# Sliding-window attention on 64-wide TensorE tiles instead of block-diagonal 128-wide operands

## Chip, cores and metric

One core of one Trainium2 chip. The metric is the device time of one execution in microseconds (us); with one core there is no slowest core to choose. Times are medians with the lowest and highest run. The *span* is the profiled part of an execution, some 2 us shorter than its time. Engines: PE is TensorE's matmuls, PEld its weight loads, DVE is VectorE, ACT ScalarE, POOL GpSimd, SP SyncE; L209 is line 209 of a kernel.

## The reference, cut to what matters

```python
# attention: 8 batches, 8 heads, 576 tokens, head size 64, window 64
scores = (q @ k^T) / sqrt(64)
mask = (rel >= 0) & (rel < 64)                   # rel = query position - key position
attn = softmax(where(mask, scores, -1e9))
x = (attn @ v).transpose(0, 2, 1, 3).reshape(4608, 512)
# feed-forward
g = x @ w_gate                                   # 512 -> 1536
out = (silu(g) * (x @ w_val)) @ w_out            # 1536 -> 512
```

A query sees at most 64 keys, so a block of 64 keys matters only to two blocks of 64 queries: its own and the next. The kernel takes the 4608 tokens in nine tiles of 512 (eight key blocks), and two heads at a time (four *pairs* per tile).

## The kernel before

Two heads share the 128 partitions. To keep them apart the keys lie block-diagonally (kbd), and so do the values (vbd): half of each 128x128 operand is zeros, written once by memsets. One matmul then gives the scores of one key block for both heads, with head on the partitions.

```python
def transposes(t, u):
    tp = ps_a.tile([P, 2, 512], BF16, name="tp", tag="a")
    # ... eight 128x128 transposes of the cast queries and keys into tp
    nc.scalar.copy(queries[t][:, u, :], tp[:, 0, :])                 # qT, ACT
    kt = tp[:, 1, :].rearrange("r (j e x) -> r j e x", j=8, e=2)
    for a in range(2):                                               # kbd, DVE, twice
        r = slice(64 * a, 64 * a + 64)
        kb = kbd[t % 2][r, u, :, r].rearrange("r j (x e) -> r j e x", e=2)
        nc.vector.tensor_copy(kb, kt[r])

def masks(t, u, eng=nc.gpsimd):
    # ... two multiplications of E by the mask, on eng
    if t < 8:
        nc.gpsimd.memset(E[:, t, 0, :], 0.0)                         # batch boundary
    F = epool.tile([P, 8, 64], BF16, name="F", tag="F")
    nc.gpsimd.tensor_add(F[:], E[:, :, 0, :], E[:, :, 1, :])         # for the denominators

def attention(t, after):            # tiles 0 and 1 only
    casts(t)
    for u in range(4):
        for g in range(2):
            cast_unit(nc.gpsimd, t, 0, g, u=u)       # q_b on POOL
            cast_unit(nc.vector, t, 1, g, u=u)       # k_b on DVE
        transposes(t, u)
        cast_v(t, u)
        if u == 3:
            after()                                  # POOL issues weight transfers
        if u:
            scores(t, u - 1)
            masks(t, u - 1, nc.vector)
        if u > 1:
            products(t, u - 2)
    # ... scores and masks of pair 3, products of pairs 2 and 3

attention(0, lambda: weights_gv(0, 384))
nc.vector.memset(kbd[1][:], 0.0)
nc.vector.memset(vbd[1][:], 0.0)
nc.vector.memset(vbd[2][:], 0.0)
for m in range(3):
    gate_value(0, m)
# ... attention(1), gate work of both tiles, then
for u in range(4):
    transposes(2, u)
    if u == 0:
        project(0, 0)
    scores(2, u); cast_v(2, u); masks(2, u, nc.vector)
    if u:
        project(0, u)
cast_qk(3)                                           # eight casts on POOL
for u in range(4):
    transposes(3, u); products(2, u); project(1, u); scores(3, u)
# ... and the steady part, t = 3 to 8:
for u in range(4):
    products(t, u)
    if u % 2 == 0:
        project(t - 1, u // 2)
for u in range(4):
    scores(t + 1, u)
    if u % 2 == 1:
        project(t - 1, 2 + u // 2)
```

tp, s_ps (scores), ad_ps (denominators) and ao_ps (products) share four PSUM banks, the pool ps_a.

The softmax here doesn't subtract the row's maximum and nothing guards it: scores larger than these inputs give would overflow.

## Time and profile before

| | before |
|---|---|
| time | 415.82 us (415.72 to 418.97, 3 runs) |
| span | 413.7 us |
| PE / DVE / ACT / POOL busy | 359.3 / 200.5 / 187.5 / 190.3 us |

The prediction shows five stretches of the table of windows, the steady tile and the chain. Two more readings are needed below. First the stretches again, cut this time at instructions that both kernels have (the gate run that waits for the last xT, the first key cast of tile 1, the first transposes after the gate work). Columns: window and length, then busy us and instruction count of PE, PEld, DVE, ACT, POOL, then granted clock (the share of TensorE's full speed that was granted), DMA share, GB/s.

```profile
0.00:36.58 36.58, 14.89 (x107) 10.04 (x108) 18.29 (x33) 12.95 (x22) 18.17 (x39) 1.00 0.77 159
36.58:46.11 9.53, 6.29 (x25) 2.49 (x24) 7.04 (x7) 3.57 (x5) 3.13 (x6) 0.83 0.36 94
46.11:73.82 27.71, 14.22 (x112) 10.41 (x112) 14.14 (x29) 11.89 (x21) 17.89 (x30) 0.50 0.96 174
...
109.43:153.54 44.11, 35.78 (x282) 20.32 (x281) 23.85 (x37) 17.73 (x32) 16.94 (x29) 0.92 0.30 90
153.54:214.14 60.60, 59.89 (x386) 31.05 (x383) 31.97 (x47) 31.95 (x52) 42.76 (x58) 1.00 0.57 127
214.14:252.39 38.25, 37.55 (x260) 19.92 (x257) 19.65 (x29) 20.89 (x34) 23.43 (x32) 1.00 0.47 111
```

They are attention of tile 0, the early gate work, attention of tile 1, then (after a PE-full stretch of 35.61 us, left out) attention of tiles 2 and 3 between projections, and two stretches where PE is full. Only the first four stretches are not bound by PE.

Second, the timelines of PE and POOL of the kernel before where tile 3 begins (start, busy us, instruction, and in brackets the idle time before it and what ended it):

```profile
128.57 4.28 PE L268 MATMUL o_ps<-wo,hT 128*128 128x512 bf16 x12
...
137.18 3.40 PE L268 MATMUL o_ps<-wo,hT 128*128 128x512 bf16 x12
```

```profile
129.66 0.15 POOL L211 MEMSET E<- 128x64 bf16 x1 [2.95 <-DVE E L209]
130.14 1.14 POOL L213 TENSOR_TENSOR F<-E 128x512 bf16<-128x512 bf16 x1 [0.34 <-DVE E L209]
131.23 0.61 POOL L118 CAST q_b<-q_f 128x512 bf16<-128x512 f32 x1
```

The projection o_ps takes 2.75 us elsewhere in this kernel; these two run partly at a halved clock (granted clock 0.50 from 128.26 to 131.67 and from 135.09 to 138.50 us). POOL waits 2.95 us for masked weights E, does a memset and F, and only then the casts on which tile 3's transposes wait.

### The profile page before, as it was taken

How to read it: one execution, taken by the hardware profiler on the slowest of the kernel's cores; microseconds unless marked ns; L12 is line 12 of the kernel's file. 1: busy time of each engine (PE TensorE's matmuls, PEld its weight loads, DVE VectorE, ACT ScalarE, POOL GpSimd, SP SyncE). 2: the span in 40 equal slices, each digit the busy share in tenths (PEclk: the TensorE clock that was granted, in tenths of full speed). 3: DMA queues.
4: the chain of work that ended last, by engine and by line, in shares of the span. 5: the costliest groups of instructions: out<-in, count | busy, mean ns of one | idle time of the engine just before them, and what ended most of it. 6: DMA issues, size and time to landing. Idle time of an engine off the chain costs nothing.

```text
span 413.7 us, 6332 instructions
## 1 busy us (share of the span) xinstructions
PE 359.3 (87%) x2296; PEld 189.2 (46%) x2296; DVE 200.5 (48%) x300; ACT 187.5 (45%) x306; POOL 190.3 (46%) x281
## 2 busy tenths in 40 slices
PE   2177445999957999999999999999999999999996
PEld 0153234444533565455455455544555554454442
DVE  4466654433453465662654456346526543343332
ACT  0355325433431465475456546644754565353320
POOL 6163269400046159769626945691599029400000
PEclk9999555999998899999999999999999999999999
DMA  8648499997010919313921671193123011002002
GB/s 213 146 93 150 109 224 158 207 225 143 16 52 26 253 67 232 87 53 106 198 53 52 174 154 50 58 251 81 36 84 86 0 52 51 2 26 78 0 2 101
DMA packets 88415, 42.89 MB, mean 104 GB/s; under 512 B 41280, under 2 KB 83776, under 8 KB 88384
## 3 DMA queue, kind: packets, MB, share of 16 engines
q1 hardware_dynamic: 78304, 36.19, 36.0%
q0 software_dynamic: 5792, 4.72, 7.4%
q10 hardware_dynamic: 4288, 1.57, 1.8%
q8 instruction: 18, 0.29, 0.3%
q14 instruction: 13, 0.11, 0.1%
HBM read 37.75 MB, written 9.44 MB: 114 GB/s over the span
## 4 chain that ended last, share of the span: by engine, by line
PE 77%; SPq 7%; DMA 7%; ACT 2%; POOL 2%; DVE 2%; issue 2%; ACTq 0%; POOLq 0%
PE g_ps L257 22%; PE v_ps L257 22%; PE o_ps L268 21%; DMA k_f<-in_k_dram 4%; PE ao_ps L233 4%; SPq L91 4%; PE tp L158 3%; PE s_ps L191 3%; SPq L101 2%; PE ad_ps L224 2%; DVE kbd L170 2%; DMA q_f<-in_q_dram 2%; ACT E L196 1%; DMA v_f<-in_v_dram 1%; SPq L86 1%
## 5 line engine op out<-in xcount | busy, mean ns | idle before, releaser
L263 DVE TENSOR_TENSOR hT<-sg,v_ps 128x512 bf16<-128x512 f32 x108 | 74.1, 687 | 92.3 <-PE v_ps L257 87.8
L257 PE MATMUL v_ps<-xT,wv 128*128 128x512 bf16 x432 | 111.7, 381 | 2.9 <-DVE hT L263 2.9
L257 PE MATMUL g_ps<-xT,wg 128*128 128x512 bf16 x432 | 112.3, 382 | 0.2 <-DVE xT L242 0.2
L262 ACT ACTIVATE sg<-g_ps 128x512 f32<-128x512 f32 x108 | 64.4, 597 | 105.3 <-PE g_ps L257 105.2
L268 PE MATMUL o_ps<-wo,hT 128*128 128x512 bf16 x432 | 100.7, 385 | 0.0
L209 POOL TENSOR_TENSOR E<-E,mask 128x512 bf16<-128x512 bf16 x48 | 54.3, 1152 | 35.0 <-ACT E L196 33.4
L170 DVE COPY kbd<-tp 64x512 bf16<-64x512 bf16 x72 | 52.2, 725 | 35.6 <-ACT qT L165 35.1
L257 PEld LDWEIGHTS <-wv 128*128 128x128 bf16 x432 | 42.3, 98 | 55.4 <-issue 4.2
L257 PEld LDWEIGHTS <-wg 128*128 128x128 bf16 x432 | 41.8, 99 | 47.4 <-issue 1.1
L268 PEld LDWEIGHTS <-hT 128*128 128x128 bf16 x432 | 40.8, 99 | 45.3 <-issue 2.8
L213 POOL TENSOR_TENSOR F<-E 128x512 bf16<-128x512 bf16 x36 | 41.6, 1156 | 16.6 <-DVE E L209 14.5
L196 ACT ACTIVATE E<-s_ps 128x512 bf16<-128x512 f32 (+1 forms) x72 | 37.7, 594 | 25.0 <-PE s_ps L191 24.9
L165 ACT COPY qT<-tp 128x512 bf16<-128x512 bf16 x36 | 21.1, 587 | 49.6 <-PE tp L158 49.6
L242 DVE TENSOR_TENSOR xT<-ao_ps,r 128x512 bf16<-128x512 f32 x36 | 26.3, 731 | 25.3 <-ACT r L241 19.6
L118 POOL CAST q_b<-q_f 128x512 bf16<-128x512 f32 x28 | 17.2, 613 | 46.1 <-PE tp L158 46.1
L158 PE MATMUL tp<-identb,q_b 128*128 128x128 bf16 x144 | 17.2, 238 | 21.1 <-POOL q_b L120 19.2
L211 POOL MEMSET E<- 128x64 bf16 x32 | 4.8, 150 | 56.5 <-DVE E L209 55.3
L233 PEld LDWEIGHTS <-vbd 128*128 128x128 bf16 x320 | 23.3, 108 | 14.6 <-issue 9.2
L239 ACT ACTIVATE ld<-ad_ps 128x512 f32<-128x512 f32 x36 | 21.6, 599 | 18.5 <-PE ad_ps L224 18.3
L191 PE MATMUL s_ps<-qT,kbd 128*128 128x128 bf16 (+1 forms) x288 | 23.9, 232 | 4.2 <-DVE kbd L170 4.1
L233 PE MATMUL ao_ps<-E,vbd 128*128 128x128 bf16 x320 | 25.6, 234 | 0.0
L191 PEld LDWEIGHTS <-kbd 128*128 128x128 bf16 x288 | 19.5, 108 | 13.1 <-DVE kbd L170 8.0
(72 smaller groups left out, 251.7 us busy)
## 6 DMA issues: line engine op xcount, KB each, us to landing
q_f<-in_q_dram SPq DMA_DIRECT2D x9, 512.0 KB, 5.0
k_f<-in_k_dram SPq DMA_DIRECT2D x9, 512.0 KB, 7.4
v_f<-in_v_dram SPq DMA_DIRECT2D x16, 112.0 KB, 2.8
v_f<-in_v_dram SPq DMA_DIRECT2D x12, 128.0 KB, 3.3
wg<-in_moe_w_gate_dram POOLq DMA_DIRECT2D x4, 384.0 KB, 8.1
wv<-in_moe_w_val_dram POOLq DMA_DIRECT2D x4, 384.0 KB, 10.2
v_f<-in_v_dram SPq DMA_DIRECT2D x16, 96.0 KB, 3.9
wo<-in_moe_w_out_dram POOLq DMA_DIRECT2D x2, 768.0 KB, 23.8
```

Source lines behind the costliest of these rows:

```text
L158: nc.tensor.transpose(tv[:, i, g, e], x[:, g, e, 2 * u:2 * u + 2, :].rearrange("r h d -> r (h d)"), identb[:],)
L170: nc.vector.tensor_copy(kb, kt[r])
L191: nc.tensor.matmul(s_ps[:, 64 + P * i:64 + P * i + n], kbd[t % 2][:, u, j, :], qT[:, 64 * j:64 * j + n],)
L196: nc.scalar.activation(Ef[:, 512 * h + lo:512 * h + 512], s_ps[:, lo:512], AF.Exp, scale=0.125)
L209: eng.tensor_mul(part, part, mf[:, lo:512])
L213: nc.gpsimd.tensor_add(F[:], E[:, :, 0, :], E[:, :, 1, :])
L233: nc.tensor.matmul(o_ps[:, lo:hi], vb, Ef[:, e0:e0 + hi - lo], start=first, stop=(j == 7), skip_group_check=True,)
L242: nc.vector.tensor_mul(xT[t][:, u, :].rearrange("r (j x e) -> r j e x", j=8, e=2), o_ps[:].rearrange("r (j e x) -> r j e x", j=8, e=2), r[ ...
L257: nc.tensor.matmul(ps[:], w[:, c, P * m:P * m + P], xT[t][:, c, :], start=(c == 0), stop=(c == 3),)
L262: nc.scalar.activation(sg[:], g_ps[:], AF.Silu)
L263: nc.vector.tensor_mul(hT[t][:, m, :], sg[:], v_ps[:])
L268: nc.tensor.matmul(o_ps[:], hT[t][:, c, P * s:P * s + P], wo[:, c, :], start=(c == 0), stop=(c == 11),)
```

## The change

The intent: use TensorE's quadrants, so that nothing is stored block-diagonally. Keys stay dense (kT, one copy); each score matmul uses 64 rows (one head) and 64 columns of TensorE (a *TensorE tile*, printed as 64*64 in the traces below; tiles that have all rows and half of the columns, printed as 128*64, are *column tiles*), and the parity of the key block decides which half of the partitions it writes. Each head then has its own PSUM bank and its keys on the partitions, two neighbouring key blocks one above the other. The products contract over all 128 partitions for a 64-query block, so the denominator is a matmul with ones, and F goes. The zero halves and their memsets go.

```diff
-    kbd = [... [P, 4, 8, P] ...]      # 2
-    vbd = [... [P, 4, 8, P] ...]      # 3
+    kT = [... [P, 4, 512] ...]        # 2
+    vp = [... [P, 9, H, D] ...]       # 2; POOL writes each value block to two slots
@@ transposes
-        nc.scalar.copy(queries[t][:, u, :], tp[:, 0, :])
-        for a in range(2): ... nc.vector.tensor_copy(kb, kt[r])
+        nc.scalar.copy(outs[0], parts[0])            # now reorders on write
+        nc.vector.tensor_copy(outs[1], parts[1])
@@ scores
-        per half: 1 + 4 matmuls with kbd[:, u, j, :], N = 64 or 128
+        for j in range(-1 if t else 0, 8):
+            c = j % 2
+            for h in range(2):
+                r = slice(64 * h, 64 * h + 64)
+                nc.tensor.matmul(s_ps[h][64 * c:64 * c + 64, lo:hi],
+                                 src[r, u, 64 * (j % 8):64 * (j % 8) + 64], qT[r, lo:hi])
+        tile 0 only: a memset and a small exponential per head for the first block
@@ masks
-        two multiplications of 512 columns
-        if t < 8: nc.gpsimd.memset(E[:, t, 0, :], 0.0)
-        nc.gpsimd.tensor_add(F[:], E[:, :, 0, :], E[:, :, 1, :])
+        one multiplication of 1024 columns
+        if 0 < t < 8:
+            a = 64 * (1 - t % 2)
+            nc.gpsimd.memset(E[a:a + 64, :, 64 * t:64 * t + 64], 0.0)
@@ products
-        nc.tensor.matmul(d_ps[:], bones[:], F)
-        9 matmuls with vbd, accumulating
+        for h in range(2):
+            nc.tensor.matmul(d_ps[64 * h:64 * h + 64, :], ones[:], E[:, h, :])
+        for m in range(8):
+            for h in range(2):
+                nc.tensor.matmul(o_ps[64 * h:64 * h + 64, 64 * m:64 * m + 64],
+                                 vp[t % 2][:, m, 2 * u + h, :], E[:, h, 64 * m:64 * m + 64])
@@ between attention of tile 0 and its gate work
-    nc.vector.memset(kbd[1][:], 0.0); nc.vector.memset(vbd[1][:], 0.0); nc.vector.memset(vbd[2][:], 0.0)
```

Value transfers change shape too, and those of tiles 0 and 1 are issued with the first pair.

More of the change, by code (lines that the diff above doesn't have):

```diff
@@ L47 @@
     wo = cst.tile([P, 12, DM], BF16, name="wo")
-    kbd = [cst.tile([P, 4, 8, P], BF16, name=f"kbd{i}") for i in range(2)]
-    vbd = [cst.tile([P, 4, 8, P], BF16, name=f"vbd{i}") for i in range(3)]
+    kT = [cst.tile([P, 4, 512], BF16, name=f"kT{i}") for i in range(2)]
+    vp = [cst.tile([P, 9, H, D], BF16, name=f"vp{i}") for i in range(2)]
     identb = cst.tile([P, P], BF16, name="identb")
-    bones = cst.tile([P, P], BF16, name="bones")
-    mask = cst.tile([P, 4, 2, 64], BF16, name="mask")
+    ones = cst.tile([P, D], BF16, name="ones")
+    mask = cst.tile([P, 2, 4, 2, 64], BF16, name="mask")
     def segments(t):
@@ L95, in load_qk, with load_v @@
                 o, s, left = o + m, s + m, left - m
-    def load_v(engs, t, p):
-        v_f = stage.tile([P, 8, D], FP32, name="v_f", tag="v_f", bufs=8)
-        for off, b, s0, n in segments(t):
-            for a in range(2):
-                engs[a].dma_start(
-                    v_f[64 * a:64 * a + 64, off // 64:(off + n) // 64],
-                    v[b, 2 * p + a, s0:s0 + n].rearrange("(j r) d -> r j d", r=64),
-                )
-        staged[t, p] = v_f
+    def load_v(engs, t, by_head=False):
+        v_f = stage.tile([P, 4, H, D], FP32, name="v_f", tag="v_f")
+        staged[t, "v"] = v_f
+        n = 0
+        for off, b, s0, left in segments(t):
+            o, s = off, s0
+            while left:
+                m = min(left, P - o % P)
+                if by_head and m == P:
+                    m = left // P * P
+                    for h in range(H):
+                        engs[h % 2].dma_start(
+                            v_f[:, o // P:(o + m) // P, h, :],
+                            v[b, h, s:s + m].rearrange("(i r) d -> r i d", r=P),
+                        )
+                else:
+                    engs[n % 2].dma_start(
+                        v_f[o % P:o % P + m, o // P],
+                        v[b, :, s:s + m].rearrange("h r d -> r h d"),
+                    )
+                n += 1
+                o, s, left = o + m, s + m, left - m
     ready = {}
@@ L130, in cast_qk, with cast_v @@
                     cast_unit(nc.gpsimd, t, i, g, e=e)
-    def cast_v(t, p):
-        v_f = staged.pop((t, p))
-        vb = vbd[t % 3]
-        nc.gpsimd.tensor_copy(vb[0:64, p, :, 0:64], v_f[0:64])
-        nc.gpsimd.tensor_copy(vb[64:128, p, :, 64:128], v_f[64:128])
+    def cast_v(t, u):
+        v_f = staged[t, "v"]
+        hs = slice(2 * u, 2 * u + 2)
+        if u == 0 and t:
+            nc.gpsimd.tensor_copy(vp[t % 2][64:128, 0], vp[(t - 1) % 2][64:128, 8])
+        for a in range(2):
+            r = slice(64 * a, 64 * a + 64)
+            dst = vp[t % 2][r, a:a + 8, hs, :].rearrange("r (i c) h d -> r i c (h d)", c=2)
+            src = v_f[r, :, hs, :].rearrange("r i h d -> r i (h d)")
+            nc.gpsimd.tensor_copy(
+                dst, src.rearrange("r i (c x) -> r i c x", c=1).broadcast_to([64, 4, 2, P])
+            )
     def weights_gv(f0, f1):
@@ L164, in transposes @@
             queries[t] = att.tile([P, 4, 512], BF16, name="qT", tag="qT")
-        nc.scalar.copy(queries[t][:, u, :], tp[:, 0, :])
-        kt = tp[:, 1, :].rearrange("r (j e x) -> r j e x", j=8, e=2)
-        for a in range(2):
-            r = slice(64 * a, 64 * a + 64)
-            kb = kbd[t % 2][r, u, :, r].rearrange("r j (x e) -> r j e x", e=2)
-            nc.vector.tensor_copy(kb, kt[r])
+        parts = [tp[:, i, :].rearrange("r (j e x) -> r j e x", j=8, e=2) for i in range(2)]
+        outs = [
+            x[:, u, :].rearrange("r (j x e) -> r j e x", j=8, e=2)
+            for x in (queries[t], kT[t % 2])
+        ]
+        nc.scalar.copy(outs[0], parts[0])
+        nc.vector.tensor_copy(outs[1], parts[1])
     weights = {}
@@ L176, in scores @@
         qT = queries[t][:, u, :]
-        E = epool.tile([P, 8, 2, 64], BF16, name="E", tag="E")
-        Ef = E[:].rearrange("r m c x -> r (m c x)")
-        for h in range(2):
-            s_ps = ps_a.tile([P, 512], FP32, name="s_ps", tag="a")
-            lo = 0
-            if t == 0 and h == 0:
-                lo = 64
-            else:
-                j = 4 * h - 1
-                kb = kbd[t % 2][:, u, j, :] if j > 0 else kbd[(t - 1) % 2][:, u, 7, :]
-                nc.tensor.matmul(s_ps[:, 0:64], kb, qT[:, 256 * h:256 * h + 64])
-            for i in range(4):
-                n = P if i < 3 else 64
-                j = 4 * h + i
-                nc.tensor.matmul(
-                    s_ps[:, 64 + P * i:64 + P * i + n],
-                    kbd[t % 2][:, u, j, :],
-                    qT[:, 64 * j:64 * j + n],
-                )
-            nc.scalar.activation(
-                Ef[:, 512 * h + lo:512 * h + 512], s_ps[:, lo:512], AF.Exp, scale=0.125
-            )
+        E = epool.tile([P, 2, 512], BF16, name="E", tag="E")
+        s_ps = [ps_a.tile([P, 512], FP32, name="s_ps", tag="a") for _ in range(2)]
+        for j in range(-1 if t else 0, 8):
+            c = j % 2
+            lo, hi = max(0, 64 * j), min(512, 64 * j + P)
+            src = kT[t % 2] if j >= 0 else kT[(t - 1) % 2]
+            for h in range(2):
+                r = slice(64 * h, 64 * h + 64)
+                nc.tensor.matmul(
+                    s_ps[h][64 * c:64 * c + 64, lo:hi],
+                    src[r, u, 64 * (j % 8):64 * (j % 8) + 64],
+                    qT[r, lo:hi],
+                )
+        for h in range(2):
+            if t == 0:
+                nc.vector.memset(E[64:128, h, 0:64], 0.0)
+                nc.scalar.activation(E[0:64, h, 0:64], s_ps[h][0:64, 0:64], AF.Exp, scale=0.125)
+            lo = 0 if t else 64
+            nc.scalar.activation(E[:, h, lo:512], s_ps[h][:, lo:512], AF.Exp, scale=0.125)
         weights[t, u] = E
@@ L203, in masks @@
         E = weights[t, u]
-        Ef = E[:].rearrange("r m c x -> r (m c x)")
-        mf = mask[:].rearrange("r m c x -> r (m c x)")
-        for h in range(2):
-            lo = 64 if t == 0 and h == 0 else 0
-            part = Ef[:, 512 * h + lo:512 * h + 512]
-            eng.tensor_mul(part, part, mf[:, lo:512])
-        if t < 8:
-            nc.gpsimd.memset(E[:, t, 0, :], 0.0)
-        F = epool.tile([P, 8, 64], BF16, name="F", tag="F")
-        nc.gpsimd.tensor_add(F[:], E[:, :, 0, :], E[:, :, 1, :])
-        weights[t, u] = (E, F)
+        eng.tensor_mul(
+            E[:].rearrange("r h x -> r (h x)"),
+            E[:].rearrange("r h x -> r (h x)"),
+            mask[:].rearrange("r h i c x -> r (h i c x)"),
+        )
+        if 0 < t < 8:
+            a = 64 * (1 - t % 2)
+            nc.gpsimd.memset(E[a:a + 64, :, 64 * t:64 * t + 64], 0.0)
     xT = {}
     def products(t, u):
-        E, F = weights.pop((t, u))
-        Ef = E[:].rearrange("r m c x -> r (m c x)")
+        E = weights.pop((t, u))
         if u == 0:
@@ L223, in products @@
         d_ps = ps_a.tile([P, 512], FP32, name="ad_ps", tag="a")
-        nc.tensor.matmul(d_ps[:], bones[:], F[:].rearrange("r m x -> r (m x)"))
+        for h in range(2):
+            nc.tensor.matmul(d_ps[64 * h:64 * h + 64, :], ones[:], E[:, h, :])
         o_ps = ps_a.tile([P, 512], FP32, name="ao_ps", tag="a")
-        first = True
-        for j in range(-1, 8):
-            if j < 0 and t == 0:
-                continue
-            vb = vbd[t % 3][:, u, j, :] if j >= 0 else vbd[(t - 1) % 3][:, u, 7, :]
-            lo, hi = max(0, 64 * j), min(512, 64 * j + P)
-            e0 = 64 * (2 * j + 1) if j >= 0 else 0
-            nc.tensor.matmul(
-                o_ps[:, lo:hi], vb, Ef[:, e0:e0 + hi - lo],
-                start=first, stop=(j == 7), skip_group_check=True,
-            )
-            first = False
+        for m in range(8):
+            for h in range(2):
+                nc.tensor.matmul(
+                    o_ps[64 * h:64 * h + 64, 64 * m:64 * m + 64],
+                    vp[t % 2][:, m, 2 * u + h, :],
+                    E[:, h, 64 * m:64 * m + 64],
+                )
         ld = fsb.tile([P, 512], FP32, name="ld", tag="ld", bufs=2)
@@ L241, in products @@
         nc.scalar.activation(r[:], ld[:], AF.Exp, scale=-1.0)
-        nc.vector.tensor_mul(
-            xT[t][:, u, :].rearrange("r (j x e) -> r j e x", j=8, e=2),
-            o_ps[:].rearrange("r (j e x) -> r j e x", j=8, e=2),
-            r[:].rearrange("r (j e x) -> r j e x", j=8, e=2),
-        )
+        nc.vector.tensor_mul(xT[t][:, u, :], o_ps[:], r[:])
     hT = {}
@@ L290, in loads_v @@
     def loads_v(t):
-        for p in range(4):
-            load_v((nc.sync, nc.sync), t, p)
+        load_v((nc.sync, nc.sync), t)
     def loads_by_head(t, e0, e1):
@@ L299, in loads_by_head @@
                 load_qk(e1, t, 1, 2 * u + a)
-            load_v((e0, e1), t, u)
+            if u == 0:
+                load_v((e0, e1), t, by_head=True)
     loads_by_head(0, nc.sync, nc.scalar)
@@ L307 @@
     make_identity(nc, identb[:])
-    nc.vector.memset(kbd[0][:], 0.0)
+    nc.vector.memset(ones[:], 1.0)
+    nc.vector.memset(vp[0][64:128, 0], 0.0)
     nc.gpsimd.memset(mask[:], 1.0)
-    nc.vector.memset(vbd[0][:], 0.0)
-    nc.vector.memset(bones[:], 0.0)
-    nc.vector.memset(bones[0:64, 0:64], 1.0)
-    nc.vector.memset(bones[64:128, 64:128], 1.0)
     for a in range(2):
-        half = mask[64 * a:64 * a + 64].rearrange("r m c (e x) -> r m c e x", e=2)
-        nc.gpsimd.affine_select(
-            out=half[:, :, 0], in_=half[:, :, 0], compare_op=ALU.is_ge, fill=0.0,
-            base=-1, pattern=[[0, 4], [-1, 2], [-2, 32]], channel_multiplier=1,
-        )
-        nc.gpsimd.affine_select(
-            out=half[:, :, 1], in_=half[:, :, 1], compare_op=ALU.is_ge, fill=0.0,
-            base=0, pattern=[[0, 4], [1, 2], [2, 32]], channel_multiplier=-1,
-        )
+        for h in range(2):
+            half = mask[64 * a:64 * a + 64, h]
+            nc.gpsimd.affine_select(
+                out=half[:, :, 1 - a], in_=half[:, :, 1 - a], compare_op=ALU.is_ge, fill=0.0,
+                base=-1, pattern=[[0, 4], [-1, 64]], channel_multiplier=1,
+            )
+            nc.gpsimd.affine_select(
+                out=half[:, :, a], in_=half[:, :, a], compare_op=ALU.is_ge, fill=0.0,
+                base=0, pattern=[[0, 4], [1, 64]], channel_multiplier=-1,
+            )
     def attention(t, after):
@@ L346 @@
     set_silu()
-    nc.vector.memset(kbd[1][:], 0.0)
-    nc.vector.memset(vbd[1][:], 0.0)
-    nc.vector.memset(vbd[2][:], 0.0)
     for m in range(3):
```

## The prediction

> **What bounds the kernel now.** I read the table of stretches first: each engine's busy time in windows, cut where the chain of waits changes character. Columns: window and length, busy us and instruction count of PE, PEld, DVE, ACT, POOL, granted clock, DMA share, GB/s.
>
> ```profile
> 0.00:35.00 35.00, 13.50 (x103) 9.52 (x104) 17.57 (x32) 11.42 (x20) 18.17 (x39) 1.00 0.75 155
> ...
> 44.00:72.56 28.56, 14.80 (x117) 10.84 (x116) 14.09 (x29) 10.65 (x20) 16.80 (x28) 0.50 0.90 168
> 72.56:109.38 36.82, 36.81 (x168) 16.42 (x167) 14.49 (x21) 14.28 (x23) 4.13 (x8) 0.99 0.90 165
> 109.38:153.00 43.62, 35.30 (x273) 19.84 (x272) 23.36 (x36) 17.66 (x31) 16.40 (x28) 0.92 0.31 91
> ...
> 253.22:291.47 38.25, 37.54 (x257) 19.90 (x256) 19.65 (x29) 20.89 (x35) 23.41 (x33) 1.00 0.43 111
> ```
>
> So there are two kernels in one. In the two stretches before 72.6 us no engine is over 60% busy: attention of tiles 0 and 1 is a chain of short steps from engine to engine. From 72.6 to 109.4, and from about 137 to the end, PE is full (37.54 of 38.25 us in a tile), and only PE work counts. Between 109.4 and about 137 PE is held up again. Second view, the timeline of PE in a steady tile:
>
> ```profile
> 217.39 0.38 PE L224 MATMUL ad_ps<-F,bones 128*128 128x512 bf16 x1
> 217.61 0.61 PE L233 MATMUL ao_ps<-E,vbd 128*128 128x64 bf16 x9
> ...
> 222.03 0.19 PE L187 MATMUL s_ps<-qT,kbd 128*128 128x64 bf16 x1
> 222.06 0.36 PE L191 MATMUL s_ps<-qT,kbd 128*128 128x128 bf16 x4
> 222.25 0.19 PE L187 MATMUL s_ps<-qT,kbd 128*128 128x64 bf16 x1
> ...
> 223.58 0.19 PE L187 MATMUL s_ps<-qT,kbd 128*128 128x64 bf16 x1 [0.70 <-ACT E L196]
> ```
>
> By start times, a head pair's denominator takes 0.22, its products 0.45, its scores 2 x 0.22 = 0.45 us; one wait of 0.70 us per tile comes in the scores. So attention's products and scores cost 4 x (0.67 + 0.45) = 4.5 of 38.25 us; the rest is FFN and transposes. Third, the chain of waits (start, us, piece) around 126 us, and the timeline of the start:
>
> ```profile
> 125.86 0.59 ACT qT L165
> 126.48 0.71 DVE kbd L170
> 127.20 0.74 DVE kbd L170
> ...
> 128.45 1.09 ACT E L196 x2
> ...
> 130.17 0.13 POOL F L213
> ...
> 131.23 0.61 POOL q_b L118
> ```
>
> ```profile
> 43.53 1.86 PE L257 MATMUL v_ps<-xT,wv 128*128 128x512 bf16 x4 [2.92 <-DVE hT L263]
> ...
> 59.08 1.15 POOL L213 TENSOR_TENSOR F<-E 128x512 bf16<-128x512 bf16 x1 [0.21 <-DVE E L209]
> ...
> 60.17 0.86 POOL L120 CAST q_b<-q_f 128x256 bf16<-128x256 f32 x2
> ```
>
> Two key copies of 0.73 us, one after the other, lie on the path of every head pair in the short-step stretches; the F add on POOL (1.15 us) stands in front of the query casts for the next pair or tile; and PE waits 2.92 us for an hT multiply that stands behind three DVE memsets of 1.76 us.
>
> [...] No tiled matmul is in this trace.[...] 0.03 us from a 64-column matmul to the next.[...]
>
> **The change, part by part.** I follow the instruction order of both kernels per engine.
>
> *Start, to 72.6 us.* ACT does its first copy at 13.05 us, after issuing its loads and a table load; unchanged. In tile 0 I redid the trace's chain with the new lengths: one key copy of 0.73 for two; no F before the next query cast; but two extra small exponentials per pair on ACT (two heads' first 64 rows; my estimate from 597 against 548 ns for 512 and 448 columns: about 0.25 each), and both heads' scores are interleaved, so the first exponential waits for both. The gain of 1.3 to 1.9 us per pair is mostly given back to ACT: I get about 1.4 us. Then three DVE memsets (3 x 1.76, with pauses to 6.4 us) vanish between tile 0's attention and its first hT: worth the 2.92 us wait and a bit, 3.3. In attention of tile 1 the loop of 5.8 us per pair (query cast at 54.41, again at 60.17) loses F and half of the key copy but keeps a POOL memset: about 1 us in each of two loops, and 0.3 in the first. At the end POOL issues the remaining weight transfers (62.20 to 68.35) before the last masks' follow-up: one F of 1.15 goes, while the value casts before it double (64x512 at 0.61 each, 2 per pair, become 64x1024, estimate 1.2 each: +1.2). Together 1.4 + 3.3 + 2.3 + about 1 = 8 us. SP issues 58 instead of 64 transfers for tile 1 (about 0.47 us each), so loads don't hold it back much, though the last keys land near when they are wanted.
>
> *Stretch 109 to 137.* Four pairs each lose 0.73 of the key copy: 2.9. The last one loses F before the eight casts for tile 3: 1.15. Back come perhaps 0.2 for the interleaved scores: about 4 us saved.
>
> *PE-bound remainder.* Scores become 18 matmuls per pair (64 rows, 64 columns of weights, N = 128 or 64) for 10; products 16 (N = 64) for 9; denominators 2 for 1: PE goes from 2296 to 2872 matmuls. The work in columns is 2 x 1024 for scores on four tiles: a perfect overlap gives 0.21 us for 0.45. Products: 1024 columns on two column tiles: 0.21 for 0.45. Denominators 2 x 512 on two: 0.22 as before. Best case 0.47 us per pair less, 1.9 per tile. If instead each load-and-matmul pair takes 27 ns whatever the tile, scores are 0.49 and products 0.43, nothing gained.[...] I choose about 20 to 24 ns: -0.6 per tile.[...] The wait at the second score pair remains, and more matmuls now stand behind it (18 instead of 5): +0.25. So +0.25 per tile, times 6 tiles of such work, +1.5 us[...].
>
> *Beside other work, no time:* the key copies from 72 to 36 (26 us of DVE), F (41.6 us of POOL) against longer value casts (+43 us), masks merged into half as many instructions of twice the length, fewer value transfers, and everything in the steady tile that isn't PE: DVE, ACT and POOL are 50 to 60% busy there.
>
> Sum: -8 - 4 + 2.5 = -9.5 us on a span of 413.7; the measured time is 2.1 us above the span: 415.8 - 9.5 = about 406.
>
> **Rivals.** (a) Tiles overlap ideally: PE saves up to 1.9 - 0.9 = 1 us per tile, 6 us more: about 398.[...] Against:[...] here each matmul has its own weight load. (b) Weight loads or a lack of overlap bind:[...] (c) The start is held by transfers (DMA share 0.75 and 0.90) and weights come too late when the start gets shorter: the 8 us shrink to 3 or 4, giving about 410. Against: in 44 to 72 the chain is engine steps, and PE waits for weights only 0.9 us in all. (d) The POOL value casts become the bound: 4 x 2.4 + 0.6 + casts 4.5 + masks 9.1 + memsets 0.6 = 24.4 us of POOL per tile, against 23.4 before in 38.25: no.
>
> **Range and chances.** The early gain is fairly sure (12, give or take 3)[...]. So 395 to 419 at 8 in 10. Faster by over 2% (below 407.5) needs a PE term below about +4: 0.57. Slower by over 2% needs rival (b) nearly in full: 0.07. The rest, 0.36.
>
> **What would show it.** In the changed profile: first gate matmul run of tile 1 (72.56 before) at about 64.5; the stretch from the end of the early gate work to the PE-full part shorter by 4 us; a tile period near 38.5 for 38.25; scores of a pair 0.3 to 0.5 us and products 0.3 to 0.45 by start times; POOL about as busy as before, DVE about 26 us less. A tile period over 40 means that loads or mode changes cost far more than I took; under 37.5 that tiles overlap nearly fully. A start that is no shorter means that the loads or ACT set it.

The sum came to -9.5 us: -8 at the start, -4 in the stretch of tiles 2 and 3, +2.5 for the rest. What a change of mode (full array to TensorE tiles or back) was taken to cost had no measurement behind it; it was part of the +0.25 per tile, of the 0.9 in rival (a) and of the +2.5, so what is printed of these does not add up. The 0.21 us of perfect overlap and the 27 ns are estimates from the trace of before: four gate matmuls of 512 columns are followed by the next group after 0.86 us, so 0.215 us each, and 27 ns for 64 columns. The 20 to 24 ns are between these 27 ns and the 12 to 13 ns that 0.21 us for 18 or 16 matmuls comes to.

## The result

| | before | after |
|---|---|---|
| time | 416.34 us (415.72 to 418.97, 4 runs) | 403.09 us (402.35 to 403.85, 4 runs) |
| span | 413.7 us | 400.5 us |
| mean granted clock | 0.955 | 0.964 |
| DVE busy | 200.5 us | 165.9 us |

The ratio is 0.967 (95% interval 0.9623 to 0.9717): faster by 3.3%. All ratios here are the mean time of one kernel's fast runs over that of the other's fast runs of the same rounds, so not quite the ratio of the quoted medians. The engine line of the page of after, and its clock by slices in tenths (40 slices of 10 us):

```profile
PE 352.9 (88%) x2872; PEld 173.4 (43%) x2872; DVE 165.9 (41%) x254; ACT 193.1 (48%) x314; POOL 186.0 (46%) x229
...
PEclk9999559999997999999999999999999999999999
```

PE runs 576 matmuls more and is busy 6.4 us less. The two slices at 5 are attention of tile 1, where PE is busy half of the time (11.84 of 23.56 us), and the 7 is the beginning of tile 3 (granted clock 0.50 from 119.27 to 126.10 us). The table of stretches of after, cut at the same instructions as that of before:

```profile
0.00:31.90 31.90, 13.40 (x171) 7.43 (x172) 13.65 (x30) 13.73 (x30) 21.49 (x38) 1.00 0.81 184
31.90:38.30 6.40, 5.91 (x25) 2.49 (x24) 1.98 (x4) 3.24 (x5) 2.82 (x4) 1.00 0.33 91
38.30:61.86 23.56, 11.84 (x175) 7.01 (x176) 11.03 (x21) 12.43 (x22) 16.24 (x27) 0.57 0.87 180
...
97.63:140.03 42.40, 34.99 (x378) 18.00 (x375) 17.13 (x25) 18.46 (x31) 15.33 (x25) 0.92 0.29 94
140.03:200.90 60.87, 59.78 (x449) 29.62 (x448) 26.96 (x40) 33.23 (x52) 41.56 (x45) 1.00 0.51 126
200.90:239.24 38.34, 37.24 (x322) 18.54 (x320) 16.65 (x25) 21.60 (x34) 22.63 (x26) 1.00 0.43 111
```

Length against length: 36.58 to 31.90 (-4.7), 9.53 to 6.40 (-3.1), 27.71 to 23.56 (-4.2), the PE-full stretch 35.61 to 35.77 (+0.2), 44.11 to 42.40 (-1.7), 60.60 to 60.87 (+0.3) and 38.25 to 38.34 (+0.1). The first three make -12.0 of the span's -13.2. A steady tile gained nothing, although its tiled matmuls did get faster. Timeline of PE in that tile of after:

```profile
204.19 0.41 PE L241 MATMUL ad_ps<-E,ones 128*64 128x512 bf16 x2
204.43 0.42 PE L245 MATMUL ao_ps<-E,vp 128*64 128x64 bf16 x16
204.68 0.39 PE L241 MATMUL ad_ps<-E,ones 128*64 128x512 bf16 x2
205.11 0.44 PE L245 MATMUL ao_ps<-E,vp 128*64 128x64 bf16 x16
205.49 2.76 PE L276 MATMUL o_ps<-wo,hT 128*128 128x512 bf16 x12
208.18 0.41 PE L241 MATMUL ad_ps<-E,ones 128*64 128x512 bf16 x2
...
210.42 0.41 PE L208 MATMUL s_ps<-qT,kT 64*64 64x64 bf16 x17 [0.96 <-ACT E L218]
210.77 2.76 PE L276 MATMUL o_ps<-wo,hT 128*128 128x512 bf16 x12
213.46 0.65 PE L208 MATMUL s_ps<-qT,kT 64*64 64x64 bf16 x36
```

Read by start times, because the busy time of a matmul group includes the latency of its last one (four gate matmuls are busy 1.03 us and the next group starts after 0.86). Products: 204.43 to 204.68, 0.25 us for 16 (before 0.45 for 9). Scores of two pairs: 213.46 to the projection at 214.04, 0.58 us for 36, a change of mode included (before 0.90 for 20). Then the costs. From a projection's start to the next tiled group it now takes 2.69 us (205.49 to 208.18) where 2.59 had been usual: each change of mode (full array, 128x64 tiles, 64x64 tiles) costs about 0.1 us (16 products take 0.25 us where the next denominators follow, 0.35 us where a projection or scores do: 201.14 to 201.49, 208.42 to 208.77), and there are nine per tile. And the wait in the scores grew from 0.70 to 0.96 us. What ends it is the first exponential of the first pair's scores, which ACT starts only behind the logarithm and the exponential of the fourth products:

```profile
209.26 0.63 ACT L253 ACTIVATE r<-ld 128x512 f32<-128x512 f32 x1
209.79 2.24 ACT L218 ACTIVATE E<-s_ps 128x512 bf16<-128x512 f32 x4
```

By steps between starts, before and after: first products with projection 3.25 and 3.29; second and third products 1.38 and 1.30; projection 2.59 and 2.69; fourth products and first two pairs of scores, wait included, 2.44 and 2.59; projection 2.59 and 2.69; last two pairs of scores 0.90 and 0.58; projection 2.59 and 2.60. Both columns add up to 15.74 us; the 0.09 us that the period grew is the change of mode after the last transposes (0.31 us to the first denominators, before 0.22).

The same view where tile 3 begins, and POOL there:

```profile
114.18 2.76 PE L276 MATMUL o_ps<-wo,hT 128*128 128x512 bf16 x12
...
122.36 4.59 PE L276 MATMUL o_ps<-wo,hT 128*128 128x512 bf16 x12
```

```profile
116.30 0.20 POOL L231 MEMSET E<- 64x128 bf16 x1 [2.76 <-DVE E L224]
116.56 0.61 POOL L132 CAST q_b<-q_f 128x512 bf16<-128x512 f32 x1
```

F is gone, but the memset stays, and it waits for E as before, so the eight casts (0.56 us from start to start) still begin only when the last mask is done: 2.38 us after the start of the projection before them (114.18 to 116.56) for 2.66 (128.57 to 131.23). And the projection at 122.36 ran partly at the low clock, 4.59 us for 3.40. The same memset is seen in attention of tile 1, in PE's and POOL's timelines of after:

```profile
58.00 0.64 PE L241 MATMUL ad_ps<-E,ones 128*64 128x512 bf16 x2 [4.28 <-POOL E L231]
```

```profile
56.02 1.69 POOL L167 DMA_DIRECT2D wo<-in_moe_w_out_dram x2
57.75 0.34 POOL L231 MEMSET E<- 64x128 bf16 x2
```

POOL issues weight transfers from 51.62 to 57.7 us and does the two 0.2 us memsets only then; PE waits 4.28 us for them. In before PE waited 4.74 us at this place, for F.

### The profile page after: what moved, and what is told of

Its sections match the earlier page's. It is cut to its first block, busy times and chain, and to the rows that moved or that the text cites. A ratio compares the mean times of both kernels' runs of the same rounds, so it can differ in the third digit from the quotient of the medians.

```text
span 400.5 us, 7241 instructions
## 1 busy us (share of the span) xinstructions
PE 352.9 (88%) x2872; PEld 173.4 (43%) x2872; DVE 165.9 (41%) x254; ACT 193.1 (48%) x314; POOL 186.0 (46%) x229
## 4 chain that ended last, share of the span: by engine, by line
PE 76%; POOL 5%; issue 5%; DMA 5%; ACT 4%; SPq 3%; DVE 1%; POOLq 0%; DVEq 0%; ACTq 0%
PE v_ps L265 23%; PE g_ps L265 23%; PE o_ps L276 22%; PE tp L180 3%; DMA v_f<-in_v_dram 3%; POOL vp L156 2%; PE ad_ps L241 2%; PE s_ps L208 2%; SPq L91 2%; PE ao_ps L245 2%; DMA k_f<-in_k_dram 2%; ACT ld L251 1%; ACT E L218 1%; SPq L109 1%; ACT L288 1%
## 5 line engine op out<-in xcount | busy, mean ns | idle before, releaser
L156 POOL CAST vp<-v_f 64x1024 bf16<-64x1024 f32 x72 | 75.4, 1047 | 16.1 <-DMA v_f<-in_v_dram 13.4
L224 POOL TENSOR_TENSOR E<-E,mask 128x1024 bf16<-128x1024 bf16 x24 | 51.0, 2124 | 32.1 <-ACT E L218 30.6
L192 ACT COPY qT<-tp 128x512 bf16<-128x512 bf16 x36 | 26.4, 734 | 39.0 <-PE tp L180 39.0
L193 DVE COPY kT<-tp 128x512 bf16<-128x512 bf16 x36 | 26.4, 732 | 37.0 <-ACT qT L192 37.0
L254 DVE TENSOR_TENSOR xT<-ao_ps,r 128x512 bf16<-128x512 f32 x36 | 24.9, 692 | 30.8 <-ACT r L253 30.8
L208 PE MATMUL s_ps<-qT,kT 64*64 64x128 bf16 (+1 forms) x640 | 17.4, 233 | 9.8 <-ACT E L218 4.8
L180 PE MATMUL tp<-identb,k_b 128*128 128x128 bf16 x144 | 16.2, 239 | 11.0 <-DVE k_b L134 11.0
L231 POOL MEMSET E<- 64x128 bf16 x28 | 5.6, 202 | 41.6 <-DVE E L224 40.4
L253 ACT ACTIVATE r<-ld 128x512 f32<-128x512 f32 x36 | 22.7, 630 | 1.2
L180 PEld LDWEIGHTS <-q_b 128*128 128x128 bf16 x144 | 10.7, 101 | 24.4 <-POOL q_b L134 14.4
```

The lines of the kernel that those rows point to most:

```text
L156: nc.gpsimd.tensor_copy(dst, src.rearrange("r i (c x) -> r i c x", c=1).broadcast_to([64, 4, 2, P]))
L180: nc.tensor.transpose(tv[:, i, g, e], x[:, g, e, 2 * u:2 * u + 2, :].rearrange("r h d -> r (h d)"), identb[:],)
L192: nc.scalar.copy(outs[0], parts[0])
L193: nc.vector.tensor_copy(outs[1], parts[1])
L208: nc.tensor.matmul(s_ps[h][64 * c:64 * c + 64, lo:hi], src[r, u, 64 * (j % 8):64 * (j % 8) + 64], qT[r, lo:hi],)
L224: eng.tensor_mul(E[:].rearrange("r h x -> r (h x)"), E[:].rearrange("r h x -> r (h x)"), mask[:].rearrange("r h i c x -> r (h i c x)"),)
```

## Experiments

Twelve kernels, all with the right result, all compared with before in the same rounds. After itself was not measured again, so the ratios to before are the fair comparison, and differences of a us in time are not. In before and after alike, ACT's two table loads per tile (1.28 us each) are clean markers; the table gives the time from marker to marker in each profile: A0 from the start to the end of tile 0's attention, G0 the early gate work as ACT sees it, A1 attention of tile 1 (with the memset wait), G the PE-full stretch, T the stretch of tiles 2 and 3, and P the steady tile.

| kernel | A0 | G0 | A1 | G | T | P | time, us | ratio (95%) |
|---|---|---|---|---|---|---|---|---|
| before | 35.79 | 5.48 | 31.75 | 36.36 | 45.14 | 38.25 | 416.34 | |
| after | 31.14 | 6.23 | 23.73 | 36.32 | 43.83 | 38.34 | 403.09 | 0.967 (0.962 to 0.972) |
| prod_by_head | 31.19 | 6.92 | 23.61 | 36.41 | 44.67 | 38.45 | 405.32 | 0.973 (0.965 to 0.981) |
| scores_by_head | 31.27 | 6.11 | 23.73 | 36.32 | 43.75 | 38.38 | 401.80 | 0.966 (0.959 to 0.972) |
| scores_moved | 31.16 | 5.43 | 23.61 | 37.34 | 45.49 | 37.13 | 397.55 | 0.954 (0.947 to 0.961) |
| before_scores_moved | 37.18 | 5.92 | 30.26 | 36.66 | 45.39 | 37.38 | 412.48 | 0.991 (0.985 to 0.998) |
| pool_step_back | 33.10 | 6.39 | 27.59 | 37.50 | 46.19 | 38.34 | 410.81 | 0.986 (0.978 to 0.994) |
| two_key_copies | 32.41 | 6.51 | 25.72 | 36.84 | 45.71 | 38.33 | 406.37 | 0.977 (0.970 to 0.984) |
| memsets_back | 31.42 | 5.91 | 26.71 | 36.32 | 43.88 | 38.33 | 406.75 | 0.977 (0.969 to 0.985) |
| loads_back | 30.68 | 7.00 | 23.61 | 36.44 | 44.21 | 38.33 | 402.58 | 0.968 (0.961 to 0.974) |
| three_back | 35.59 | 5.46 | 33.48 | 36.32 | 50.59 | 38.32 | 421.61 | 1.014 (1.010 to 1.018) |
| before_memsets_early | 36.14 | 6.21 | 27.73 | 36.35 | 49.61 | 38.25 | 416.83 | 1.002 (0.997 to 1.008) |
| memset_on_dve | 31.32 | 6.90 | 21.06 | 37.66 | 39.30 | 38.32 | 396.25 | 0.954 (0.951 to 0.958) |
| moved_and_dve | 31.08 | 5.59 | 19.74 | 37.64 | 39.29 | 37.12 | 389.03 | 0.937 (0.932 to 0.941) |

Each row of intervals is one profiled execution. How far they repeat is seen where the code up to there is the same: the end of A1 comes at 73.02 and 73.36 us in before and before_scores_moved, at 61.10, 61.11 and 60.20 us in after, scores_by_head and scores_moved. The medians of before were 416.56, 415.18 and 414.81 us.

### Do column tiles overlap, and is it worth anything? (prod_by_head, scores_by_head)

The theory: products and scores run at once on alternating tiles, and the order of the matmuls makes that possible. The rival: PE's gain is there, but waits absorb it.

```diff
-        for m in range(8):
-            for h in range(2):
+        for h in range(2):
+            for m in range(8):          # products: neighbours share a column tile
```

> The changed kernel with the products of one head first and then those of the other, so that eight matmuls in a row go to the same column tile. Theory (the 0.25 us that a pair's 16 products take in the changed kernel, for 0.45 before, comes from two column tiles running at once): products take 0.45 us or more per pair again, the steady tile of 38.34 us becomes 39.1 us or longer, the time 403 becomes 407 to 409 us. Rival (short matmuls simply follow each other every 15 ns, whatever the tile): period and time unchanged within 0.1 us and 0.3%.

The PE timeline of the steady tile of prod_by_head:

```profile
202.84 0.57 PE L245 MATMUL ao_ps<-E,vp 128*64 128x64 bf16 x16
203.34 2.76 PE L276 MATMUL o_ps<-wo,hT 128*128 128x512 bf16 x12
```

The first products take 0.50 us to the projection, 0.40 without the mode change, for 0.35 in after (201.14 to 201.49), 0.25 without it. So overlap is real: 25 ns per matmul with neighbours on one column tile, 15.6 ns when two tiles alternate. Both are means. In the single records of after (products of the steady tiles) the starts come in pairs, 3 to 4 ns apart on the two column tiles, then 25 to 29 ns to the next pair; in prod_by_head most are 25 to 33 ns apart. But the tile period rose by 0.11 us only, where four times 0.15 is 0.6: only the first pair's 0.15 shows. The step of the second and third products took 1.26 us for 1.30, and that of the fourth with its wait 2.59 for 2.59 (210.0 to 212.6 us), so there the overlap lies in front of waits. The theory held in kind and fell in size (38.45 us against 39.1 or more, 405.32 us against 407 to 409). Of the 2 us in the total, part is in G0 and T.

```diff
-        for j in range(-1 if t else 0, 8):
-            ...
-            for h in range(2):
+        for h in range(2):
+            for j in range(-1 if t else 0, 8):   # scores: all of head 0 first
```

> The changed kernel with the 9 score matmuls of one head first and then those of the other: neighbours still alternate the column tile, but no longer the row tile and the bank. Theory (all four tiles run at once, rows and columns): half of the overlap goes, scores of a pair take about 0.45 us for 0.25, tile period 38.34 becomes about 39.1 us, time about 406 to 408 us. Rival (two column tiles alone give the whole gain[...]): no change.

The last 36 score matmuls took 0.63 us for 0.58, the tile period 38.38 for 38.34: the order of heads hardly matters to scores. Here neighbours still alternate between column tiles (the parity of the key block), which fits; the theory that the interleaving of heads was needed fell.

### What holds the steady tile? (scores_moved, before_scores_moved)

The theory: the wait before the second pair's scores, where a shared bank comes free only after ACT's logarithm and exponential of the fourth products, takes PE's gain. A projection between each two pairs of scores covers it.

```diff
             for u in range(4):
                 if t + 1 < NT:
                     scores(t + 1, u)
-                if u % 2 == 1:
+                if u % 2 == 0:
                     project(t - 1, 2 + u // 2)
```

> The changed kernel with the third and fourth projection put after the first and third score group instead of after the second and fourth, so that the second group's banks are free when its turn comes. Theory (PE waits 0.96 us per tile for a bank of the products' last pair, and a change of tile mode costs about 0.1 us): the wait goes, two more mode changes come, tile period 38.34 becomes about 37.6 us, five tiles have it: time about 399 to 400 us. Rival (the wait only moves to another place, because ACT sets the pace with its two table loads, logarithms and exponentials): period within 0.2 us of 38.34.

> The same move of two projections in the kernel before, which has no tile modes. Theory: its wait of 0.70 us goes and nothing comes in its place, tile period 38.25 becomes about 37.55 us, time 416 becomes about 412.5 us. Then the 64-wide tiles are worth about nothing per steady tile with or without the wait, because mode changes take what the overlap gives. Rival (the wait of 0.96 us is what hides the gain of the tiles): the changed kernel with the move comes out 0.3 us per tile or more below this one.

The PE timeline of scores_moved:

```profile
209.36 0.42 PE L208 MATMUL s_ps<-qT,kT 64*64 64x64 bf16 x18
209.71 2.76 PE L276 MATMUL o_ps<-wo,hT 128*128 128x512 bf16 x12
212.41 0.65 PE L208 MATMUL s_ps<-qT,kT 64*64 64x64 bf16 x36
212.98 2.76 PE L276 MATMUL o_ps<-wo,hT 128*128 128x512 bf16 x12
215.68 0.42 PE L208 MATMUL s_ps<-qT,kT 64*64 64x64 bf16 x18
```

No score group has a wait any more. The period fell to 37.13 us, 1.21 less, more than expected; the same edit in before gave 0.87 (37.38). With the wait gone from both, after's tile is 0.25 us shorter than before's. So the section's theory holds, and what was put for before_scores_moved (nothing gained with or without the wait) fell, its rival (0.3 us or more) being nearly met: the tiles are worth 0.25 us per steady tile, and in the change as made a wait took it. The periods carry this, since they repeat within 0.01 us from tile to tile; the totals also hold the clock in G and T.

### Where did the start come from? (pool_step_back, two_key_copies, memsets_back, loads_back, three_back)

Each puts one removed step back into after, with nothing else changed: a POOL step as long as F (an idempotent multiplication by the 0/1 mask), a second key copy, three memsets of 4096 columns on DVE, the order of value loads.

```diff
+        nc.gpsimd.tensor_mul(E[:, 0, :], E[:, 0, :], mask[:, 0]...)          # pool_step_back, in masks
-        nc.vector.tensor_copy(outs[1], parts[1])                             # two_key_copies
+        for a in range(2):
+            nc.vector.tensor_copy(outs[1][64*a:64*a+64], parts[1][64*a:64*a+64])
+    for i in range(3): nc.vector.memset(junk[:], 0.0)                        # memsets_back, before gate_value(0, m)
-            if u == 0: load_v((e0, e1), t, by_head=True)                     # loads_back
+            load_v((e0, e1), t, by_head=True, u=u)                           # two heads with each pair
```

> The changed kernel (403.1 us, gate work of tile 1 reached at 61.9 us for 73.8 before) with a POOL instruction as long as the removed F add (half of the mask applied a second time, 1.15 us, same result) in F's old place. Theory (F stood between the masks and the next query casts, so POOL waited for DVE in each loop): attention of tile 0 gets 3 to 4 us longer, of tile 1 about 3, the stretch before tile 3's casts 1.2: time 409 to 411 us. Rival (POOL is busy only half of the time and catches up; the gain came from the key copies): 403 to 405 us.

> The changed kernel with its key copy of 128 partitions cut into two of 64, as before. Theory (each costs 0.73 us whatever its partitions, and it lies on the path from transposes to scores): 0.73 us more for each of the 12 pairs of tiles 0 to 2, nothing in the steady tiles, where DVE has room: about 7 us, less what waits for something else: 407 to 410 us. Rival (the path at the start runs over POOL and the loads): at most 1 us in tiles 0 and 1, 2.9 in tile 2: 405 to 406 us.

> The changed kernel with three DVE memsets of 1.76 us (of a tile that nothing reads) where the kernel before cleared its block-diagonal tiles, between attention of tile 0 and its first gate work. Theory: PE waits again for the first hT multiply, about 3 us: 405.5 to 406.5 us. Rival (tile 1 waits for its loads anyway, so the delay is absorbed): under 1 us.

> The changed kernel with the values of tiles 0 and 1 loaded pair by pair between the queries and keys, as before, instead of all of them after the first pair's. Theory (the last load that ACT issues lands earlier in the new order, and ACT's first copy starts at 11.64 us for 13.05): ACT's first copy moves back by about 1.4 us and the end with it: 404 to 405 us. Rival (the order of loads matters more through the value casts and tile 1's keys, which now come later): no change or a gain.

> The changed kernel with all three parts put back together: the 1.15 us POOL step, the key copy in two, the three memsets; the 64-wide tiles stay. Alone they cost 9.5, 5.9 and 2.9 us of span. Theory (the gain is these three, all at the start and in tile 2's stretch, and the tiles give nothing): the whole difference comes back, at least 13 us: time 416 us or more, up to 421 if the parts add up fully. Rival (the tiles shorten the start too, so something of the gain stays): 408 to 413 us.

From the table, against after: the POOL step (1.16 us each) costs +2.0 in A0 and +3.9 in A1; the second key copy (a mean of 725 ns on 64 partitions in before, for 732 on 128 in after) +1.3 and +2.0; the memsets +3.0 in A1, and the wait of before returns in PE's timeline of memsets_back:

```profile
39.38 1.02 PE L266 MATMUL v_ps<-xT,wv 128*128 128x512 bf16 x4 [2.70 <-DVE hT L272]
```

The order of loads is worth nothing (402.58 us). To the end of A1 the three add up alone to 5.98 + 3.54 + 2.94 = 12.5 us (markers: 67.08, 64.64 and 64.04 us for 61.10), together to 13.4 (74.53), and the change gained 11.9 there (73.02 to 61.10). So these three parts are enough for the whole start gain. The surplus of 1.5 us is not far above the spread of such markers (up to 0.9 us); whether something else in the change costs time, such as ACT's reordering qT copy (0.73 us for 0.59) or the value casts, was not tested. Of what was expected, the memsets, the total of the POOL step and three_back came out about as theory said; the key copies cost less than theory and more than the rival said (406.37 us, with 1.3 and 2.0 us in A0 and A1), and the theory on the order of loads fell. In full, three_back is slower than before, mostly through its T of 50.59 us. That is the subject of the next part.

### A gain that did not arrive (before_memsets_early)

If the memsets alone cost 3 us, moving them in before to a time when DVE is free should give 3 us.

```diff
             transposes(t, u)
+            if t == 0 and u == 0:
+                clear_later()           # the three memsets, moved here
 ...
-    nc.vector.memset(kbd[1][:], 0.0); nc.vector.memset(vbd[1][:], 0.0); nc.vector.memset(vbd[2][:], 0.0)
```

> The kernel before with only its three later memsets moved to where DVE idles for 7.5 us (after the first key cast, before ACT's first copy at 13.05 us). Theory: the 2.92 us wait of PE for the first hT multiply goes: about 3 us, 413 us. Rival (tile 1 then waits for its loads): under 1 us.

The total did not move (1.002). The markers show that the gain was there and went: at the end of A1 the kernel is 2.94 us ahead of before (70.08 for 73.02), at the end of G 2.95 (106.43 for 109.38), and after T 1.52 behind. Timeline of PE in T of before_memsets_early:

```profile
113.87 4.44 PE L268 MATMUL o_ps<-wo,hT 128*128 128x512 bf16 x12
...
121.71 3.98 PE L268 MATMUL o_ps<-wo,hT 128*128 128x512 bf16 x12
...
128.73 2.75 PE L268 MATMUL o_ps<-wo,hT 128*128 128x512 bf16 x12
```

In before the same three projections took 2.75, 2.75 and 4.28 us, and the 4.28 lay in the shadow of the casts. The projection after the casts took 4.61 for 3.40. The excess on the path is 1.69 + 1.23 + 1.21 = 4.1 us of T's +4.5. What sets the clock is not shown: the instructions around these projections are the same in both kernels, yet the granted clock in T is 0.86 for 0.92, and the stretches at 0.50 in it last 3.41, 3.41 and 6.83 us (in before 3.41 and 3.41). So 3 us at the start can be lost again in T by which projections meet the low clock. Whether an earlier start makes this more likely, or it was chance, is not settled: one profile each. Of the four executions one took 412.90 us, about the 413 expected, and three 416.71 to 417.61. It also means that the T column of the kernels above holds clock beside their edit: the projections in three_back's T hold 4.5 us of it, those in after's 1.8.

### The memset that stayed (memset_on_dve, moved_and_dve)

In after the batch-boundary memset on POOL stands in front of the casts and waits for E. On DVE, which multiplies the mask in these tiles, it simply follows that multiplication, and POOL is free of E.

```diff
-            nc.gpsimd.memset(E[a:a + 64, :, 64 * t:64 * t + 64], 0.0)
+            (nc.vector if t < 3 else nc.gpsimd).memset(
+                E[a:a + 64, :, 64 * t:64 * t + 64], 0.0
+            )
```

> The changed kernel with the small clearing of E in tiles 1 and 2 on DVE, just behind the mask, in place of POOL. Theory (POOL in its fixed order still ties query casts to DVE's masks in tiles 1 and 2, and its 6 us of weight issues stand before the last two clearings, for which PE waits 4.28 us): the attention of tile 1 gets 4 to 6 us shorter, and tile 3's casts no longer wait for tile 2's last mask, up to 4 us more: time 393 to 398 us. Rival (the loads of tile 1 are issued until 45 us and hold it): gain under 2 us.

POOL's timeline of memset_on_dve:

```profile
50.05 1.70 POOL L167 DMA_DIRECT2D wo<-in_moe_w_out_dram x2
51.79 0.74 POOL L132 CAST q_b<-q_f 128x512 bf16<-128x512 f32 x1
...
113.64 0.61 POOL L132 CAST q_b<-q_f 128x512 bf16<-128x512 f32 x1 [24.66 <-issue]
```

The casts start at 113.64 us for 116.56 without waiting for E, and tile 3's transposes follow the projections at once. PE there:

```profile
103.73 4.44 PE L278 MATMUL o_ps<-wo,hT 128*128 128x512 bf16 x12
...
115.66 2.76 PE L278 MATMUL o_ps<-wo,hT 128*128 128x512 bf16 x12
...
119.42 2.76 PE L278 MATMUL o_ps<-wo,hT 128*128 128x512 bf16 x12
```

From the fourth projection to the fifth it is 3.76 us for 8.18 (114.18 to 122.36 in after), which is 4.4 of T's 4.5 us; the other steps cancel. The low clock only moved: the fifth projection takes 2.76 us for 4.59, the second 4.44 for 2.76. A1 falls by 2.7 us, T by 4.5; G and G0 give back 2.0. Of this G's 1.3 is the clock again: its first 3.51 us ran at 0.50, in after the first 0.15. In all 0.954 of before, within what was expected.

> Both repairs in the changed kernel: two projections moved (397.5 us alone) and the clearing on DVE. They act in different stretches, so they should add: 5.5 us plus what the clearing gives alone, 387 to 393 us. If less, one of them only shifts a wait.

Both edits together: 389.03 us (386.71 to 390.63), ratio 0.937. Against after (403.09) that is 14.1 us less; the two edits alone gave 5.5 and 6.8. They work in different stretches (A1 and T; P) and add up, within the 2 us that executions differ. This is the fastest kernel: the change is worth 3.3%, with two schedule edits on top 6.3%. The move of projections was worth 0.9% in before without the change; the memset edit was not tried in before, where F would still stand on POOL.

## Why the prediction was right, and where not

**Direction and size: right.** 406 predicted, 403.09 measured, inside 395 to 419. The sum was -9.5 us, the span fell by 13.2; a start that gave more and a second stretch that gave less partly cancel, which is luck. The signs named in advance: tile 1's first gate run starts at 59.85 us (72.37 before, which the prediction has as 72.56; 8 us earlier was expected, it is 12.5), the tile period is 38.34 (near 38.5), POOL is 4.3 us less busy (about the same), DVE 34.6 less (26 from the key copies alone).

**Start: under-sized, -8 against -12.0.** Its terms:
- *Tile 0's attention, -1.4 against -4.7.* "Mostly given back to ACT" failed. The extra small exponentials are busy 0.21 us each, but the next activation starts 0.11 us after one, so a pair costs 0.2 us, not 0.5. And POOL drops out of tile 0's mask step altogether (F and memset both), so query casts no longer wait for E: pool_step_back puts this at 2.0 us, two_key_copies the key copy at 1.3. The remaining 1.4 fits the step "first copy at 13.05 us, unchanged": it ran at 11.64. It is no accident of one profile: the first copy starts at 13.05, 13.38 and 14.41 us in the three profiles without the change, at 11.61 to 12.13 in the eleven with it; and before_scores_moved, which is the same as before up to there, has A0 longer by as much as its copy is later (1.39 and 1.36 us). Putting the load order back did not undo it (12.13 us). That run has the old order with the new shape of value transfers: ACT spends 1.62 us on issuing its four of them (0.37 to 0.49 us each, on 128 partitions), for 2.50 before (0.60 to 0.69 us each, on 64), and its copy comes 0.92 us earlier than before's. So most goes with the shape; for the rest no run tells order from chance.
- *The memsets, -3.3 against -3.1; putting them back cost 2.9.* Right.
- *Tile 1's attention, -3.3 against -4.2.* Right in direction. The sum's last "about 1" does not follow from its own terms, one F of 1.15 us less and 1.2 us more of value casts. The loop keeps "a POOL memset", and it comes behind the transfers at the end, as said; what this costs was not said: PE waits 4.28 us for it there, and with the memset on DVE A1 was 2.7 us shorter.

**Tiles 2 and 3: over-sized, -3 in net (-4, and a term that is cut) against -1.7.** The key copies came as predicted: the first three steps from projection to projection shortened by 0.95, 0.67 and 0.82 us (2.44 together, for four key copies' 2.9 less the mode changes of about 0.1 us each). "The last one loses F before the eight casts: 1.15" failed: the casts start 0.28 us earlier relative to the projection before them. From the end of the last exponential to the first cast it is 1.11 us for 1.69, since the memset remains, now behind one mask of 1024 columns (0.69 us); and the exponentials themselves start 0.30 us later against the projection (the prediction allowed 0.2 for interleaved scores). And the projection after them lost 1.2 us to the clock.

**Steady part: the sum about right (+0.1 per tile against +0.25), the parts wrong, so the sum is luck.** Overlap was to be worth 0.6; products and scores each fell from 0.45 to about 0.25 us per pair, more than twice that. Mode changes cost about 0.1 us each; the forecast's own figure had no measurement behind it. And the wait was to grow by what stands behind it (0.25); it grew by 0.26, but for another reason: ACT sets when the bank comes free, 2.22 us after the fourth denominator's start in before (221.36 to 223.58) and 2.24 in after (208.18 to 210.42), so whatever PE saved in between became waiting. scores_moved shows it.

**Rivals.** (a), ideal overlap, is nearly true of PE (0.25 us for an ideal 0.21, itself an estimate from the 0.215 us of a 512-column gate matmul) and untrue of the time. (b), weight loads that bind, is refuted: 15.6 ns per load and matmul, although each product has a weight load of its own (2872 loads for 2872 matmuls). (c), transfers: the order did not matter, and memset_on_dve took 2.7 us more out of A1 without a wait of PE for weights. (d), POOL's casts as the bound: no; they took 1.05 us, not 1.2, and POOL was 186.0 us busy for 190.3.

## What to carry to other kernels

Before counting on a removed instruction, look for what still stands at its place in that engine's order: at tile 3 a 0.2 us memset that waits for the same data kept POOL's casts back nearly as long (2.38 us after the projection's start) as the memset and the 1.15 us addition had (2.66). PE, made faster in front of a wait that ACT ended, gained nothing here (38.34 us per tile for 38.25) until the wait was filled with other work (37.13 for 37.38), so move such a wait first. And judge a gain of 1% or less from its own stretch of the trace as well as from the total: in before_memsets_early the 2.9 us gained at the start were gone after T, whose projections took 4.1 us longer at the low clock.
